# Transposing q and k' on TensorE instead of by DMA, in low-rank attention followed by a GELU MLP

## The chip, the cores and the metric

The kernel runs on one core of a Trainium2 chip. A core has five engines that work side by side, each with its own queue of instructions: TensorE (PE in the profile; its weight loads are the row PEld), VectorE (DVE), ScalarE (ACT), GpSimd (POOL) and SyncE (SP). Sixteen DMA engines move data; here they are fed from the queues of SP and POOL, and once from ACT's. Matmuls write into PSUM, which has 8 banks. The metric is the device time of one execution in microseconds (us), smaller is better.

## The reference

Eight batches of attention with 8 heads, 1024 tokens and head size 64. Keys and values are first projected along the sequence from 1024 to 64 by two matrices E and F, so that each head has only 64 keys. The result goes through an MLP with the sigmoid form of GELU.

```python
k_proj = np.einsum('ks,bhsd->bhkd', E, k)          # (8, 8, 64, 64), "k'"
v_proj = np.einsum('ks,bhsd->bhkd', F, v)
scores = (1/8) * np.matmul(q, k_proj.transpose(0, 1, 3, 2))
attn = softmax(scores)
x = np.matmul(attn, v_proj)                        # then (8192, 512): heads side by side
h = x @ w_in                                       # 512 -> 2048
out = (h * sigmoid(1.702 * h)) @ w_out             # 2048 -> 512
```

## The kernel before, in words

The 8192 tokens are cut into 16 blocks of 512 (`j`), two to a batch (`b`). A block passes through these steps, and the short names are those of the written order:

- `ld` and `lq` load k, v and q of a batch from POOL's queue, with the change of type to bf16 on the way (`load_kv` L58, `load_q` L70).
- `pj` projects k and v of a batch (L674); `kb` and `vq` copy the two results out of PSUM.
- `qd` and `kd` transpose q and k' of a batch by DMA transposes from SP's queue (L239, L684), so that the head size lies along the partitions, as the scores need it. `qda` and `qdb` do the same for half a batch.
- `sc` computes scores from the transposed q and k' (through `eight`, L249), `ex` the exponential on ScalarE, `su` the sums (L652), `va` the products with v' (L249). The sums go through `den`, `ga`, `rc`, `sr` and `sb`: to memory, back, inverted and broadcast over the partitions (`rbc`), with four small or middling DMAs from SP's queue. `mv` multiplies the products with them into `xT` (L646).
- `u0` to `u3` with `P1` to `P7` are the first matrix of the MLP (L610), done by Strassen's scheme with 7 products in place of 8; `c` and `d` are its copies and sums, `g` its GELUs. `xs`, `gs` are sums of its inputs. `F1` to `F7` are the second matrix by the same scheme (L504), with `Fc`, `Fo` and `Fd` behind them; `st` stores the output.

Blocks 0 and 1 go another way in the opening: block 0 has its own functions (`scores0`, `tok0`, `x_tr0`, `ffn1`, then `O` for the second matrix), block 1 has `tk`, `tr`, `tm`, `xt`, `xc` for its attention and `L`, `Lg` for the first matrix, both without Strassen's scheme. While block 0 waits for data, `warm` matmuls on zeros fill TensorE's queue. The second half of batch 0's q is transposed on TensorE by `q_tr` (L230).

What stands in which order on each engine is written out by hand, in lists of step names. `OPEN` covers the start up to block 4, `STEPS` is repeated for each block from 4 to 12, `TAIL` ends it. In `OPEN` and `TAIL` a word is name@block, with PSUM banks behind a colon and the engine of the copy behind a slash; in `STEPS`, `name+3` is that step of the block three further on. `BANK` and `ON_ACT` give banks and copying engine where a word has none. Waits follow from the data: an instruction waits for those whose results or buffers it needs, and holds up what is behind it on its engine. Steps that belong to a batch run only for even blocks (`BATCH`).

Two tiny copies on POOL into `held` put its queue on hold: in `ld` it waits for the transposed q (L677), in `lq` for `rbc` (L696), so that the large loads start only then.

Of the kernel before, what the change touches and what calls it, by code (L numbers as in the profile page):

```python
# [10 lines left out]
BF16 = mybir.dt.bfloat16  # L11
# [6 lines left out]
def kernel(ctx, tc, q, k, v, E, F,  # L18
                                                     moe_w_in, moe_w_out, out):
    nc = tc.nc  # L20
# [69 lines left out]
    for i in range(8):  # L90
        load_w_in(i)
    load_q(0, JB)
    for i in range(4):
        sl = slice(i * FC // 4, (i + 1) * FC // 4)
        nc.gpsimd.dma_start(out=w_out_sb[:, sl, :], in_=w_out_v[:, sl, :])
# [127 lines left out]
    def q_tr(g):  # L223
        def go():
            if 0 not in qT:
                qT[0] = att.tile([P, J, HP, P], BF16, name="qT")
            t_ps = f_tile([P, 2, HP, P], BF16)
            for jj in range(2):
                for p in range(HP):
                    nc.tensor.transpose(t_ps[:, jj, p, :],  # L230
                                        qt[0][:, 2 * g + jj, 2 * p:2 * p + 2, :].rearrange("s t d -> s (t d)"), ident)
            nc.vector.tensor_copy(qT[0][:, 2 * g:2 * g + 2], t_ps)
        return go

    def q_dma(b, j0=0, n=J):
        def go():
            if j0 == 0:
                qT[b] = att.tile([P, J, HP, P], BF16, name="qT")
            nc.sync.dma_start_transpose(out=qT[b][:, j0:j0 + n].rearrange("r j p s -> r (j p) s"),  # L239
                                        in_=qt[b][:, j0:j0 + n].rearrange("s j h d -> s (j h d)"))  # L240
        return go
# [67 lines left out]
    def ffn1(j, fc, ts=slice(0, TB)):  # L309
        if j not in gts:  # L310
            gts[j] = gT
        n = ts.stop - ts.start
        h_ps = f_tile([P, n])
        for kc in range(KC):
            nc.tensor.matmul(h_ps, w_in_sb[:, kc, fc * P:(fc + 1) * P], xT[j][:, kc, ts],
                             start=(kc == 0), stop=(kc == KC - 1))
        nc.scalar.activation(gts[j][:, fc, ts], h_ps, AF.Gelu_apprx_sigmoid)
# [58 lines left out]
    def ffn2_ops(j):  # L376
# [8 lines left out]
        wi.5@1/D sc.1@1:5,6 sc.0@1:7,4 ex.0.0@1 ex.1.1@1 ex.0.1@1 O.2.0@0:3 O.3.0@0:2 O.2.1@0 tk.0.1@1:0 qda@2  # L385
        O.3.1@0 ex.1.0@1 tk.0.0@1:5 tr.0.1@1 tm.0.1@1 tk.1.0@1:0 tk.1.1@1:7 tr.0.0@1 tm.0.0@1 O.1.0@0:6 O.1.1@0
        O.1.2@0 xt.0@1:4 gt@6 tr.1.0@1 tk.3.0@1:1 tr.1.1@1 tm.1.1@1 O.3.2@0 O.3.3@0 tk.2.1@1:5 tk.2.0@1:7
        xc.0@1/A wi.4@1 O.1.3@0 tm.1.0@1 tr.2.0@1 xt.1@1:0 tm.2.0@1 oc.3@0/D ws.1@1 tr.3.0@1 xc.1@1/A O.0.0@0:7
        ws.0@1 O.0.1@0 O.2.2@0 tk.3.1@1:4 tr.2.1@1 tm.2.1@1 O.0.2@0 tm.3.0@1 tr.3.1@1 tm.3.1@1 oc.1@0/D xt.2@1:5
        xc.2@1/A O.0.3@0 xt.3@1:1 xc.3@1/A O.2.3@0 ws.2@1 L.5@1:0 L.0@1:6 oc.0@0/D L.15@1:2 Lg.0@1 oc.2@0/A  # L390
        Lg.5@1 gt@3 L.4@1:4 L.1@1:7 pj@2:5 Lg.4@1 L.14@1:0 kb@2/A Lg.15@1 L.11@1:1 Lg.14@1 Lg.1@1 kd@2 L.2@1:6
        L.7@1:4 ws.3@1 L.9@1:3 vx.0@2 vq.0@2/D vx.1@2 vq.1@2/D Lg.7@1 Lg.11@1 ws.4@1 qdb@2 Lg.9@1 L.6@1:5
        L.8@1:4 L.10@1:7 Lg.8@1 Lg.2@1 L.3@1:1 L.12@1:3 L.13@1:2 ws.5@1/D lq@2 Lg.10@1 Lg.3@1 Lg.6@1 Lg.12@1
        Lg.13@1 gs1.0@1 sc.1@3:3,6 sc.0@2:0,1 gs2.0@1 sc.0@3:4,7 F1.0@1:2 ex.1.1@3 ex.0.1@2 gs1.1@1 gs4.0@1
        F1.1@1 gs2.1@1 gs3.0@1 Fc1@1:1/D F5.0@1:5 ex.1.0@3 ex.0.1@3 F5.1@1 F6.0@1 ex.0.0@3 ex.0.0@2 su@3:0,6
        den.0@3/A sc.1@2:3,4 tk.0.0@2:7 F2.1@1 ex.1.0@2 tk.1.0@2:0 ex.1.1@2 Fc3@1/A den.1@3/D tr.0.0@2 tm.0.0@2
        gs4.1@1 tk.0.1@2:3 tr.1.0@2 tm.1.0@2 tr.0.1@2 tm.0.1@2 tk.1.1@2:7 tr.1.1@2 F2.0@1 tm.1.1@2 F6.1@1 s0.1@0
        tk.2.1@2:4 tk.2.0@2:0 xt.0@2:6 s0.0@0 xt.1@2:3 F3.1@1 tr.2.1@2 tr.2.0@2 xc.0@2/A tm.2.0@2 tm.2.1@2 ga@3
        gs3.1@1 tk.3.0@2:0 F3.0@1 xc.1@2/A tk.3.1@2:6 tr.3.0@2 Fc2@1/A xt.2@2:3 tm.3.0@2 xc.2@2/A tr.3.1@2
        tm.3.1@2 gt@4 Fo0@1/A rc@3 xs.0@2 Fd2@1 F7.1@1 u0.P1@2:7 u0.c1@2:5/D xt.3@2:3 u1.P5@2:6 u1.P1@2:0  # L400
        u1.c1@2:2/D F7.0@1 xc.3@2/A xs.1@2 u0.P2@2 Fd1@1 u0.P5@2:4 u0.c3@2/D sr@3 u1.P2@2 u0.P6@2 u1.P6@2 F4.0@1
        u1.c3@2/D u0.c2@2/D u1.P3@2 ld@2 u2.P1@2:3 u0.g11@2 u3.P1@2:7 xs.2@2 u1.c2@2/A qd@4 u1.P7@2 u1.d2@2
        u1.g11@2 xs.3@2 F4.1@1 u0.P3@2 u1.g12@2 u2.c1@2:0/A sb@3 u1.d1@2 u2.P2@2 u0.d2@2 Fo1@1/A u3.c1@2:6/A
        u0.P7@2 u3.P2@2 u3.P5@2:4 u2.P5@2:1 u3.P6@2 u2.P6@2 u0.d1@2 u1.g22@2 u3.c3@2/D u3.P3@2 u3.g11@2 u0.g22@2
        u0.g12@2 pj@4:7 u3.c2@2/A u2.c3@2/A gs1.0@2 u3.P7@2 u2.g11@2 u3.d2@2 u2.c2@2/D gs3.0@2 gs2.0@2 u2.P7@2
        u1.P4@2 u3.g12@2 u2.P3@2 kb@4/A u3.d1@2 u0.P4@2 kd@4 u2.d1@2 F1.0@2:3 u1.g21@2 u2.d2@2 F1.1@2 u2.g22@2
        u3.g22@2 u2.g12@2 vq.1@4/A u0.g21@2 gs1.1@2 u3.P4@2 u2.P4@2 vq.0@4/A Fc1@2:1/A u3.g21@2 u2.g21@2
        va.1@3:2,7 va.0@3:4,5 gs2.1@2 mv.1.0@3 mv.0.0@3 F6.1@2 F2.0@2 mv.0.1@3 xs.0@3 mv.1.1@3 F2.1@2 sc.1@4:4,5
        sc.0@4:2,0 F6.0@2 ex.1.1@4 xs.1@3 gs3.1@2 Fc2@2/D F5.0@2:7 st1@1 st0@1 Fo0@2/D ex.0.1@4 ex.0.0@4
        ex.1.0@4 F5.1@2 F7.1@2 sc.0@5:3,6 sc.1@5:0,5 ex.0.0@5 su@4:4,2 den.1@4/A gs4.0@2 F7.0@2 ex.0.1@5  # L410
        den.0@4/D Fc3@2/D u0.P1@3:2 u1.P5@3:3 u0.P5@3:4 ex.1.0@5 u0.c1@3:6/A u1.P1@3:0 u0.c3@3/A gs4.1@2 xs.2@3
        u0.P6@3 Fd1@2 u0.c2@3/D F3.0@2 u1.c3@3/D ex.1.1@5 gt@2 ga@4 u1.c1@3:5/D u0.P3@3 F3.1@2 Fd2@2 u1.P6@3
        gt@5 u0.d2@3 rc@4 u1.c2@3/A ld@4 u0.P2@3 xs.3@3 u1.P2@3 u0.P7@3 u0.g11@3 F4.1@2 u1.P3@3 u1.P7@3 u0.d1@3
        u0.P4@3 u2.P1@3:7 F4.0@2 u1.d2@3 su@5:4,3 sr@4 u1.g11@3 pj@6:0 u1.d1@3 sb@4 Fo1@2/D u3.P1@3:2 u1.g12@3
        u1.P4@3 den.0@5/A u1.g22@3 u0.g22@3 den.1@5/D u2.c1@3:3/A u0.g12@3 kb@6/D u2.P6@3 u0.g21@3 gs1.0@3
        gs2.0@3 u2.P5@3:1 u3.P5@3:6 u3.c1@3:4/A vq.0@6/A u2.c3@3/A u3.c3@3/D u3.P6@3 u2.P2@3 u2.c2@3/A u2.P3@3
        gs3.0@3 vq.1@6/A u3.c2@3/A u3.P3@3 u2.g11@3 lq@4 u2.d2@3 u3.P2@3 u3.g11@3 u2.P7@3 u1.g21@3 u3.d2@3
        u3.P7@3 u3.d1@3 u3.g12@3 u2.g12@3 va.0@4:2,0 va.1@4:1,6 u2.d1@3 mv.0.1@4 mv.0.0@4 u2.g22@3 u3.g22@3
        F1.0@3:5 F1.1@3 u3.P4@3 kd@6 u3.g21@3 ga@5 gs1.1@3 u2.P4@3 mv.1.0@4 u2.g21@3 Fc1@3:1/A gs2.1@3 mv.1.1@4
        u1.P1@4:7 F5.0@3:0 u1.c1@4:6/A qd@6 xs.0@4 F5.1@3 rc@5 F6.1@3 F2.1@3 F2.0@3 u1.P2@4 u1.g11@4 F6.0@3  # L420
        sc.0@6:7,3 sc.1@6:4,2 ex.1.0@6 st1@2 xs.1@4 sr@5 u1.P6@4 xs.2@4 st0@2 xs.3@4 gs3.1@3 gs4.1@3 Fc3@3/D
        sb@5 gs4.0@3 ex.1.1@6 F3.0@3 F3.1@3 u1.c2@4/A Fc2@3/D Fo0@3/D ld@6 ex.0.0@6 F7.0@3 u1.P5@4:4 F7.1@3
        u1.P7@4 u2.P1@4:7 u1.c3@4/D ex.0.1@6 u0.P1@4:2 u1.P3@4 u0.P5@4:5 u0.c1@4:3/A gt@7 Fd1@3 Fd2@3 u0.P6@4
        u1.d2@4 u3.P1@4:0 u0.c3@4/D u0.c2@4/D u3.c1@4:4/A u0.P2@4 u1.g12@4 u0.P3@4 u0.g11@4 u0.d2@4 F4.0@3
        u3.P6@4 F4.1@3 u3.P2@4 u1.d1@4 u3.c2@4/D gt@1 u3.g11@4 u0.P7@4 Fo1@3/A u0.d1@4 u1.g22@4 u0.g22@4
        u2.P5@4:2 u1.P4@4 u2.c1@4:5/D u3.P5@4:0 u3.P7@4 u3.c3@4/D u2.P6@4 u1.g21@4 u0.g12@4 u2.c3@4/A u0.P4@4
        u3.d1@4 u3.P3@4 u3.P4@4 u2.c2@4/D u0.g21@4 u2.P2@4 u3.g21@4 u2.g11@4 u3.d2@4 u2.P7@4 u2.P3@4 va.0@5:0,3
        su@6:1,4 den.0@6/A u2.d1@4 den.1@6/A u2.g22@4 mv.0.1@5 u2.d2@4 va.1@5:6,7 u2.P4@4 u3.g12@4 gs1.0@4 lq@6
        u2.g21@4 st0@3
    """.split()  # L430
    STEPS = """
        F1.0 pj+4 mv.1.1+1 u3.g22 mv.0.0+1 u2.g12 mv.1.0+1 xs.0+1 gs2.0 ga+2 sc.1+3 sc.0+3 kb+4 F1.1 u1.P1+1
        vq.0+4 vq.1+4 gs1.1 xs.1+1 gs2.1 Fc1 kd+4 ex.1.1+3 u1.P5+1 F2.1 ex.1.0+3 u1.c3+1 F2.0 Fo0 xs.3+1 F6.0
        u1.c1+1 gs3.1 F5.0 u0.P5+1 u1.P6+1 F6.1 st1-1 ex.0.0+3 ex.0.1+3 gt+4 rc+2 sr+2 u0.P1+1 sb+2 qd+4 ld+4
        lq+3 u0.c1+1 xs.2+1 F5.1 u1.P3+1 gs3.0 Fc2 gs4.1 u0.c3+1 u0.P2+1 u1.c2+1 u1.d2+1 gs4.0 F7.0 u1.P2+1
# [40 lines left out]
    def step(name, j, banks=(), eng=None):  # L476
# [217 lines left out]
        elif i == "lq":  # L694
            if b >= 2:
                nc.gpsimd.tensor_copy(held[:, 0], rbc[j - 1][:1, 0, :1])  # L696
            load_q(b + 1)
        else:
            raise KeyError(name)
# [98 lines left out]
```

## Time and profile before

| What | us |
|---|---|
| Timed runs | 464.88, 466.00, 466.42; median 466.0 |
| Profiled execution, its own time | 464.02 |
| its span, first to last instruction | 462.2 |
| TensorE, busy | 455.6 |
| VectorE, busy | 343.6 |
| ScalarE, busy | 307.8 |
| GpSimd, busy | 82.5 |

How to read the profile: matmuls follow one another in a pipeline, and the mean duration of one (219 ns for 128 columns, 273 for 256) is longer than the distance from one start to the next. What one costs in a full queue is read from the starts. A view of waits lists the engine and line that waited, what it waited for, the time in total, how often, and the longest. In the timeline and in the chain of waits a row has the start and the duration in us, then engine, line and what was done; `x8` are eight instructions in a row. The stages' rows have start and end, length, the busy time of PE, PEld, DVE, ACT and POOL with their instruction counts, the granted clock, and the mean share and the GB/s of DMA.

DMA in the profiled execution, from the page: the software queue (POOL's loads) took 56.7% of the 16 engines' span, the hardware queue of SP 34.5%. DMA transposes: 8 of q (11.7 us from issue to landing) and 7 of k' (3.3 us).

### The profile page before, as it was taken

To read this page: it belongs to the slowest core of one execution; us is meant where nothing else is said; L and a number is where in the kernel's file an instruction comes from. 1 tells how busy PE (TensorE), PEld (TensorE's weight loads), DVE (VectorE), ACT (ScalarE), POOL (GpSimd) and SP (SyncE) were. 2 spreads that over 40 slices of the span, in tenths; PEclk is the share of its full clock that TensorE was granted. 3 is DMA by queue.
4 is the path that set the end of the run, shared out by engine and by line. 5 is a ranking of instruction groups with operands and counts; after the bars stand their busy time and mean duration, and the time that the engine had idled before them with its cause. 6 is when DMAs were issued, how large, how long until landed. Compare 5 with 4: busy or idle time off the path is not lost.

```text
span 462.2 us, 10631 instructions
## 1 busy us (share of the span) xinstructions
PE 455.6 (99%) x4378; PEld 361.9 (78%) x4378; DVE 343.6 (74%) x616; ACT 307.8 (67%) x539; POOL 82.5 (18%) x111
## 2 busy tenths in 40 slices
PE   8999999999999999999999999999999999999997
PEld 4644448877778788887888788787888888888886
DVE  4547957887785977878687876888788796977771
ACT  2665367686767967769585776958677676737462
POOL 7463107052013201041010601015000000000000
PEclk9999999999999999999999999999999999999999
DMA  9999999999999978999988987989664123242022
GB/s 167 200 187 207 182 174 156 197 241 199 148 219 254 158 145 135 223 127 157 162 152 188 156 126 143 211 158 155 138 128 116 45 79 88 94 94 92 1 91 92
DMA packets 133731, 69.19 MB, mean 150 GB/s; under 512 B 98484, under 2 KB 123060, under 8 KB 133684
## 3 DMA queue, kind: packets, MB, share of 16 engines
q0 software_dynamic: 86496, 29.37, 56.7%
q1 hardware_dynamic: 47108, 38.90, 34.5%
q8 instruction: 34, 0.56, 0.5%
q10 hardware_dynamic: 80, 0.26, 0.2%
q14 instruction: 13, 0.11, 0.1%
HBM read 72.88 MB, written 16.99 MB: 194 GB/s over the span
## 4 chain that ended last, share of the span: by engine, by line
PE 87%; DMA 8%; DVE 2%; POOL 1%; issue 1%; ACT 0%; SPq 0%; DVEq 0%; POOLq 0%; ACTq 0%
PE k_ps L504 39%; PE k_ps L610 35%; PE k_ps L249 3%; PE k_ps L550 3%; PE k_ps L556 3%; DMA v_sb<-in_v_dram 3%; PE k_ps L674 2%; DMA w_in_sb<-in_moe_w_in_dram 2%; DMA rbc<-rdr 2%; DMA rdr<-rc 1%; DVE sg L357 1%; PE k_ps L652 1%; POOL k_sb L58 0%; POOL v_sb L58 0%; PE k_ps L567 0%
## 5 line engine op out<-in xcount | busy, mean ns | idle before, releaser
L504 PEld LDWEIGHTS <-sg 128*128 128x128 bf16 x960 | 93.6, 98 | 12.0 <-issue 1.3
L610 PEld LDWEIGHTS <-late 128*128 128x128 bf16 x896 | 87.4, 98 | 11.3 <-issue 1.2
L489 DVE TENSOR_TENSOR q_even<-k_ps,q_even 128x512 f32<-128x512 f32 x112 | 74.6, 687 | 22.7 <-PE k_ps L610 21.0
L610 PE MATMUL k_ps<-xw,late 128*128 128x256 bf16 x672 | 90.2, 273 | 0.0
L504 PE MATMUL k_ps<-tw,sg 128*128 128x256 bf16 x720 | 89.1, 273 | 0.0
L626 ACT ACTIVATE gT<-k_ps 128x512 bf16<-128x512 f32 x112 | 63.8, 596 | 32.8 <-PE k_ps L610 32.2
L504 PEld LDWEIGHTS <-gT 128*128 128x128 bf16 x720 | 68.7, 98 | 15.9 <-issue 8.2
L626 ACT ACTIVATE gT<-q_even 128x512 bf16<-128x512 f32 x112 | 66.2, 630 | 19.1 <-DVE q_even L489 19.0
L610 PEld LDWEIGHTS <-w_in_sb 128*128 128x128 bf16 x672 | 65.5, 98 | 9.3 <-issue 1.7
L610 PE MATMUL k_ps<-xT,w_in_sb 128*128 128x256 bf16 x448 | 64.7, 273 | 0.5 <-DVE xT L646 0.4
L504 PE MATMUL k_ps<-w_out_sb,gT 128*128 128x256 bf16 x480 | 59.3, 273 | 0.0
L70 POOL DMA_DIRECT2D q_sb<-in_q_dram x56 | 49.0, 901 | 40.5 <-DMA qT<-q_sb 18.1
L374 DVE TENSOR_TENSOR sg<-gT 128x1024 bf16<-128x1024 bf16 x60 | 40.9, 681 | 6.6 <-ACT gT L626 3.3
L614 ACT COPY k_ps<-k_ps 128x512 f32<-128x512 f32 x40 | 23.0, 575 | 22.7 <-PE k_ps L610 20.5
L646 DVE TENSOR_TENSOR xT<-k_ps,rbc 128x512 bf16<-128x512 f32 x52 | 32.8, 683 | 3.7 <-PE k_ps L249 1.4
L489 DVE TENSOR_TENSOR o_sb<-k_ps,u_sb 128x512 f32<-128x512 f32 (+1 forms) x31 | 20.6, 668 | 19.1 <-PE k_ps L504 14.4
L638 ACT ACTIVATE expT<-k_ps 128x512 bf16<-128x512 f32 x60 | 32.4, 602 | 3.1 <-PE k_ps L249 3.0
L610 PE MATMUL k_ps<-xT,late 128*128 128x256 bf16 x224 | 33.3, 273 | 0.0
L610 PE MATMUL k_ps<-xw,w_in_sb 128*128 128x256 bf16 x224 | 31.6, 273 | 0.0
L504 PE MATMUL k_ps<-w_out_sb,sg 128*128 128x256 bf16 x240 | 30.6, 273 | 0.0
L504 PE MATMUL k_ps<-tw,gT 128*128 128x256 bf16 x240 | 29.1, 273 | 0.0
L618 DVE COPY q_even<-k_ps 128x512 f32<-128x512 f32 x37 | 25.2, 683 | 5.2 <-PE k_ps L610 5.1
(122 smaller groups left out, 522.3 us busy)
## 6 DMA issues: line engine op xcount, KB each, us to landing
out_dram<-o_sb SPq DMA_DIRECT2D x30, 512.0 KB, 5.0
rbc<-rdr SPq DMA_DIRECT2D x26, 512.0 KB, 6.2
k_sb<-in_k_dram POOLq DMA_DIRECT2D x7, 1024.0 KB, 12.3
q_sb<-in_q_dram POOLq DMA_DIRECT2D x56, 128.0 KB, 6.6
v_sb<-in_v_dram POOLq DMA_DIRECT2D x7, 1024.0 KB, 17.5
w_in_sb<-in_moe_w_in_dram POOLq DMA_DIRECT2D x8, 256.0 KB, 11.3
w_out_sb<-in_moe_w_out_dram POOLq DMA_DIRECT2D x4, 512.0 KB, 11.5
v_sb<-in_v_dram POOLq DMA_DIRECT2D x4, 256.0 KB, 10.4
```

What stands on the lines that cost most here:

```text
L70: nc.gpsimd.dma_start(out=qt[b][:, j], in_=qv[:, j])
L249: nc.tensor.matmul(outs[i][r.start + c:r.start + c + w], lhsTs[i][ri, c:c + w], rhss[i][ri], start=True, stop=True)
L374: nc.vector.tensor_tensor(t[i - 1], in0, in1, op=ALU.add if i == 1 else ALU.subtract)
L489: nc.vector.tensor_tensor(out_, in0, in1, op=ALU.add)
L504: nc.tensor.matmul(dst, x[:, k_, t * P:(t + 1) * P], w[:, k_], start=(first and k_ == 0), stop=(final and k_ == FH - 1), skip_group_check= ...
L550: nc.tensor.matmul(live[f"O{n}", j], gts[j][:, fc, n * P:(n + 1) * P], w_out_sb[:, fc, :], start=(fc == 0), stop=(fc == FC - 1))
L610: nc.tensor.matmul(live[h, j][:, r], a[:, k_, f:f + P], w[:, k_], start=(i in (1, 5) and r == 0 and k_ == 0), stop=(i in (2, 3, 4) and r = ...
L614: copy(new(B_, [P, 2, TH]), live[A, j])
L618: copy(u2, live[G, j])
L626: nc.scalar.activation(out_, in_, AF.Gelu_apprx_sigmoid)
L638: nc.scalar.activation(expT[j][:, 2 * n + t, :], live[f"S{n}{t}", j], AF.Exp, scale=scale)
L646: nc.vector.tensor_tensor(x_of(j)[:, n, :], live[f"V{p[1]}{t}", j], rbc[j][:, n, :], op=ALU.mult)
```

## The change

q and k' of batches 1 to 7 are transposed by matmuls with the identity matrix. `qt.0` and `qt.1` transpose the q of one block, 8 transposes of 128x128 each into one PSUM bank, and `qc.0`, `qc.1` copy them to `qT`, which is now kept per block. `kt` transposes k' of a batch with 4 transposes, and `kc` copies it to `kts`; `kb` now copies all 128 partitions of the projection. `qd`, `qda`, `qdb` and `kd` are gone, and with them the hold in `ld`; the hold in `lq` is now on the newest `rbc`. `q_tr` writes block 1's part alone. The three lists, the banks and the copying engines are written anew. In the opening, the last eighth of w_in is loaded behind the second half of q; ffn1's first two tiles are begun while the last heads are still missing; the sums of w_in are made in two halves. The end stores its second half in one piece.

```diff
-    for i in range(8):
+    for i in range(7):
         load_w_in(i)
     load_q(0, JB)
+    load_w_in(7)
...
-    def q_dma(b, j0=0, n=J):
-        def go():
-            if j0 == 0:
-                qT[b] = att.tile([P, J, HP, P], BF16, name="qT")
-            nc.sync.dma_start_transpose(out=qT[b][:, j0:j0 + n].rearrange("r j p s -> r (j p) s"),
-                                        in_=qt[b][:, j0:j0 + n].rearrange("s j h d -> s (j h d)"))
...
+    def ffn1_kc(fc, kc):
+        if fc not in begun:
+            begun[fc] = f_tile([P, TB]), []
+        begun[fc][1].append(kc)
+        nc.tensor.matmul(begun[fc][0], w_in_sb[:, kc, fc * P:(fc + 1) * P], xT[0][:, kc, :],
+                         start=(kc == 0), stop=(kc == KC - 1))
+
+    def ffn1_begin(fc0, fc1, n):
+        for fc in range(fc0, fc1):
+            ffn1_kc(fc, n - 1)
...
     OPEN = """
-        wi.5@1/D sc.1@1:5,6 sc.0@1:7,4 ex.0.0@1 ex.1.1@1 ex.0.1@1 O.2.0@0:3 O.3.0@0:2 O.2.1@0 tk.0.1@1:0 qda@2
...
+        O.3.0@0:7 wi.4@1 sc.1@1:2,6 sc.0@1:1,0 ex.0.1@1 ex.0.0@1 O.2.0@0:3 O.2.1@0 O.3.1@0 tk.1.0@1:5 ex.1.0@1
...
+        ws.1@1 O.1.3@0 xc.2@1/A xc.3@1/A O.0.3@0 L.6@1:5 L.7@1:7 L.8@1:3 oc.1@0/D L.2@1:4 Lg.7@1 Lg.8@1 Lg.6@1
+        qt.0@2:6 pj@2:2 oc.0@0/A qc.0@2/A vq.0@2/D L.5@1:5 L.1@1:0 L.11@1:7 L.0@1:3 vq.1@2/A gt@4 Lg.2@1 Lg.5@1
...
     STEPS = """
-        F1.0 pj+4 mv.1.1+1 u3.g22 mv.0.0+1 u2.g12 mv.1.0+1 xs.0+1 gs2.0 ga+2 sc.1+3 sc.0+3 kb+4 F1.1 u1.P1+1
-        vq.0+4 vq.1+4 gs1.1 xs.1+1 gs2.1 Fc1 kd+4 ex.1.1+3 u1.P5+1 F2.1 ex.1.0+3 u1.c3+1 F2.0 Fo0 xs.3+1 F6.0
-        u1.c1+1 gs3.1 F5.0 u0.P5+1 u1.P6+1 F6.1 st1-1 ex.0.0+3 ex.0.1+3 gt+4 rc+2 sr+2 u0.P1+1 sb+2 qd+4 ld+4
...
-        u3.P2+1 u2.d1+1 Fd2 u3.P7+1 u0.P4+1 u2.g22+1 u2.P4+1 u3.g11+1 u0.g21+1 u3.d1+1 u2.P3+1 u3.P4+1 va.0+2
-        u2.g21+1 u3.d2+1 u2.d2+1 mv.0.1+2 su+3 u3.g21+1 va.1+2 den.0+3 den.1+3 u3.g12+1 st0
+        F1.0 u3.g22 F1.1 qt.0+3 u3.g21 mv.1.1+1 qt.1+3 u3.g12 kt+3 mv.0.0+1 Fc1 F2.1 u2.g12 qc.0+3 kc+3 pj+4
+        qc.1+3 sc.0+3 lq+2 gs1.1 gs2.1 gs3.1 xs.0+1 ga+2 sc.1+3 F2.0 u0.P1+1 F6.1 vq.0+4 gs3.0 F6.0 kb+4
+        ex.1.0+3 u1.P1+1 vq.1+4 gs4.0 ex.1.1+3 ex.0.0+3 u0.c1+1 xs.1+1 Fo0 u1.P5+1 ex.0.1+3 u0.P5+1 rc+2 F5.0
...
+        u3.P7+1 u2.P4+1 su+3 ld+3 u3.d2+1 u2.g22+1 va.1+2 va.0+2 den.1+3 u3.d1+1 den.0+3 u2.g21+1 mv.1.0+2
+        u3.P4+1 mv.0.1+2
...
     TAIL = """
-        gs4.1@15 Fo0@15/A st0h@15 F4.1@15 F4.0@15 f3.1@15 f3.0@15 Fo1@15/A st4.1@15 fd2.1@15 st2.1@15 fd2.0@15
-        st2.0@15
+        Fd1@15 fd2.0@15 F4.1@15 F4.0@15 f3.1@15 st0h@15 st2.0@15 fd2.1@15 Fo1@15/A st1@15 st2.1@15
...
-    ON_ACT = ("Fc1", "Fc2", "den.0", "den.1", "kb", "u0.c1", "u0.c2", "u1.c1", "u2.c1", "u2.c3", "u3.c2", "vq.0",
-              "vq.1")
+    ON_ACT = ("Fc1", "Fc2", "Fc3", "Fo0", "den.1", "u0.c2", "u0.c3", "u1.c1", "u1.c2", "u2.c1", "u2.c3", "u3.c2",
+              "u3.c3")
...
         elif i == "ld":
-            nc.gpsimd.tensor_copy(held[:, 1], qT[b][:1, J - 1, 0, :1])
...
         elif i == "kb":
-            tmps["kb"] = att.tile([KP, H, D], BF16, name="k_b")
-            copy(tmps["kb"], live["PJ", j][LO])
-        elif i == "kd":
-            nc.sync.dma_start_transpose(out=kts[b % 2], in_=tmps["kb"].rearrange("k h d -> k (h d)"))
+            tmps["kb"] = att.tile([P, H, D], BF16, name="k_b")
+            copy(tmps["kb"], live["PJ", j])
+        elif i == "kt":
+            new("KT", [P, HP, P], BF16)
+            for n in range(HP):
+                nc.tensor.transpose(live["KT", j][:, n], tmps["kb"][:, 2 * n:2 * n + 2].rearrange("k t d -> k (t d)"),
+                                    ident)
+        elif i == "kc":
+            copy(kts[b % 2], live["KT", j][:, :, :KP])
+        elif i == "qt":
+            if j not in qT:
+                qT[j] = att.tile([P, HP, JB, P], BF16, name="qT")
+            new(f"Q{t}", [P, 2, JB, P], BF16)
+            for e in range(2):
+                for n in range(JB):
+                    nc.tensor.transpose(live[f"Q{t}", j][:, e, n],
+                                        qt[b][:, c * JB + n, 4 * t + 2 * e:4 * t + 2 * e + 2]
+                                        .rearrange("s t d -> s (t d)"), ident)
+        elif i == "qc":
+            copy(qT[j][:, 2 * t:2 * t + 2], live[f"Q{t}", j])
...
         elif i == "lq":
             if b >= 2:
-                nc.gpsimd.tensor_copy(held[:, 0], rbc[j - 1][:1, 0, :1])
+                nc.gpsimd.tensor_copy(held[:, 0], rbc[max(rbc)][:1, 0, :1])
...
+    x_tr0(2, 0, 2, AC)
     tok0(3, 0)
     tok0(3, 1)
-    warm(1, True)
-    x_tr0(2, 0, 2, AC)
+    ffn1_begin(0, 2, 1)
+    ffn1_begin(0, 2, 2)
     x_tr0(3, 0, 1, DV)
     x_tr0(3, 1, 1, AC)
...
+    ffn1_begin(0, 2, 3)
+
+    halves = slice(0, DH // 2), slice(DH // 2, DH)
+    for fc in range(FC):
+        ffn1(fc)
+        if fc in (8, 13):
+            for i in (2, 3, 0, 1):
+                w_in_sums(i, cols=halves[fc > 8])
+        if fc in (11, 12):
+            q_tr(fc - 9)()
```

## The prediction

> **What bounds the kernel now.** I read the page first, then whom TensorE waits for, then the chain of waits over one batch, the busy time by stage, and TensorE's timeline where the change touches it. The page (parts 1 and 2) shows TensorE busy almost everywhere at the full clock, and the DMA engines busy too for two thirds of the span:
>
> ```profile
> PE 455.6 (99%) x4378; PEld 361.9 (78%) x4378; DVE 343.6 (74%) x616; ACT 307.8 (67%) x539; POOL 82.5 (18%) x111
> PE   8999999999999999999999999999999999999997
> PEclk9999999999999999999999999999999999999999
> DMA  9999999999999978999988987989664123242022
> ```
>
> Since the ends of matmuls are modelled, I asked whether TensorE waits. Its list of waits is short, 2.8 us in all, and only the second line lies after the first 21 us:
>
> ```profile
> PE k_ps L144 <- DVE u_sb L109: 1.5, 1, 1.5
> PE k_ps L610 <- DVE xT L646: 0.4, 1, 0.4
> PE k_ps L184 <- DMA v_sb<-in_v_dram: 0.4, 1, 0.4
> ```
>
> The chain of waits over one batch is matmuls only. From one batch's projection to the next (210.27 to 264.11) are 53.84 us, and 8 matmuls of 256 columns take 0.87 us, 109 ns each. The stages (PE, PEld, DVE, ACT, POOL, clock, DMA share, GB/s) say that this pace does not depend on the DMA engines: a share of 0.96 or of 0.61 makes no difference.
>
> ```profile
> 210.27 1.85 PE k_ps L674 x16
> 212.12 0.56 PE k_ps L249 x16
> ...
> 264.11 1.85 PE k_ps L674 x16
> ```
>
> ```profile
> 210.30:264.10 53.80, 53.80 (x546) 45.12 (x548) 42.23 (x73) 38.89 (x68) 9.10 (x12) 1.00 0.96 158
> 317.90:371.80 53.90, 53.90 (x553) 45.22 (x560) 42.14 (x73) 38.99 (x68) 0.09 (x1) 1.00 0.61 114
> ```
>
> So TensorE's queue is full from 22 us to the end. What is added to it lengthens the kernel one for one, and what is taken off the DMA engines gives nothing unless a TensorE wait goes with it. One rule says otherwise: the Trainium skill, "Perfetto Trace Analysis", section Identifying the Most-Contended Engine, calls matmul busy time a bad measure and has headroom judged by the weight loads' busy share. By it, 78% would leave 22% of 462 us, some 100 us, in which transposes could hide. I follow the starts instead: they stand 109 ns apart with no holes.
>
> **The change part by part.** *Transposes added.* Each block from 2 to 15 (14 of them) gets `qt.0` and `qt.1`, 8 transposes each: 224. Each batch from 1 to 7 gets `kt`, 4 transposes: 28. In sum 252 of 128x128 bf16. The trace has the same operation, `q_tr` at L230:
>
> ```profile
> 34.09 0.61 PE L230 MATMUL k_ps<-ident,q_even 128*128 128x128 bf16 x8
> 34.54 1.03 PE L315 MATMUL k_ps<-xT,w_in_sb 128*128 128x512 bf16 x4
> 35.40 0.61 PE L230 MATMUL k_ps<-ident,q_even 128*128 128x128 bf16 x8
> 35.85 1.03 PE L315 MATMUL k_ps<-xT,w_in_sb 128*128 128x512 bf16 x4
> 36.97 0.63 PE L249 MATMUL k_ps<-qT,kt 64*32 64x512 bf16 x16
> ```
>
> Eight occupy TensorE from 34.09 to 34.54, 56 ns each; the 219 ns that the groups give as mean is latency, not pitch. 252 x 0.0556 = 14.0 us. Two rules of the Trainium skill, "TensorE: Matmul & The Clock Gate", speak against the change more strongly. Part 4 (PE-mode transpose) gives about 275 ns per transpose inside a kernel: 69 us. Part 2 (Back-to-back issue gap) gives 81 ns for 128 columns with a weight load each: 20.4 us. The row is of this kernel, with weight loads, so 14.0 is taken; 20.4 stays as the upper end, and no row supports 69.
>
> *Groups of split matmuls.* Projection, scores, values and sums use parts of the array, and entering such a group costs: the 8 matmuls of L610 should give way at 417.48 + 0.87 = 418.35, but L249 starts at 418.44, 0.09 us later.
>
> ```profile
> 417.48 1.04 PE L610 MATMUL k_ps<-xw,late 128*128 128x256 bf16 x8
> 418.44 0.62 PE L249 MATMUL k_ps<-expT,vq 64*32 64x512 bf16 x16
> ```
>
>  Counting unbroken groups in the orders: OPEN 12 before, 16 after; TAIL 1 and 2; STEPS 2 and 2 (one holds `pj`). Five more, 0.5 us. The other matmuls are the same in kind and number, but for one `warm` of 512 columns that goes (it is in the opening's sum).
>
> *Opening.* Before ffn1, TensorE's timeline is:
>
> ```profile
> 19.53 0.62 PE L184 MATMUL k_ps<-v_sb,late 128*128 128x128 bf16 x8 [0.35 <-DMA v_sb<-in_v_dram]
> 20.93 0.38 PE L144 MATMUL k_ps<-zeros 128*128 128x512 bf16 x1
> 21.95 12.30 PE L315 MATMUL k_ps<-xT,w_in_sb 128*128 128x256 bf16 x64
> ```
>
> The last `v` lands at 19.5 us in both, since its loads are issued first. Before, TensorE then has waits and a `warm` until L315 starts at 21.95 and ffn1 ends at 35.85 + 4 x 0.216 = 36.71. After, six of ffn1's 64 matmuls (1.3 us) are begun in those waits. Worked along DVE's and ACT's copies, the last x_tr0 is copied at about 22.5, then 58 x 0.216 + 0.9 (q_tr) = 13.4: ffn1 ends at 35.95, so 0.75 less. The scores of block 1 also stand 0.26 behind ffn1 (36.71 to 36.97), waiting for q_tr's copies on DVE, which trail the sums of w_in (L357, waits of 7.7 us on w_in's DMA); the new place of those sums and `O.3.0` ahead of the scores cover that. Together -1.0. `load_w_in(7)` moved behind four q loads lands where the last of those did, near 33.5 us; its first user, fc = 14, comes near 34.2. Nothing, but with 0.7 us of cover.
>
> *Waits that go.* At 130.4 TensorE stands 0.6 us for xT (L646), behind rbc's DMAs that share SP's queue with transposes; at 382.6 it stands 0.2. Both go with luck: -0.8.
>
> *Waits that come, in the opening.* In TensorE's order `pj@2` now stands after all O, the tk and xt, four L and `qt.0`: 35.95 + 13.8 + 0.65 + 0.9 + 0.9 + 3.45 + 0.45 = 56.1. It needs v of batch 1, issued at 39.11 and 18.3 us to landing, 57.4; before, `pj` began at 57.57. Nothing ahead of that load gets lighter. So +1.0, with 12 L matmul groups queued behind it. `pj@4` is as tight (k and v of batch 2, issued near 60 and after 14 us, against 74.5): 0 to 1.5, taken as 0.
>
> *Waits that come, in the steady order.* `sc.0` and `sc.1` need `qc.0`, `kc`, `qc.1` from DVE, where a 128x1024 copy is 680 ns (L232). In odd blocks, where no `pj` stands between, TensorE has qt.1 0.45 + kt 0.22 + F2.1 0.87 = 1.5 us between qt.0 and sc.0. DVE has, from va's end, the last of u3.d1, den.0, four mv (2.48 us for four), qc.0, kc: about 4.3 us against TensorE's 4.2 up to sc.0, and qc.1 0.6 later. From nothing to 0.6 us a block; taken 0.2 in the five odd blocks, +1.0; the bad end is 0.5 in all twelve, 6.
>
> *Copies.* 28 qc and 7 kc make per batch 4 x 0.68 + 0.3 = 3.0 us on DVE; `ON_ACT` moves five copies a block to ScalarE and den.0, u0.c1, kb and vq to DVE. DVE 42.2 - 6.9 + 4.3 + 3.0 = 42.6, ScalarE 38.9 + 2.2 = 41.1, of a batch of 55.8. Both stay under TensorE: nothing.
>
> *Queues.* SP loses 8 q and 7 k' transposes (landing 11.7 and 3.3 us); behind them stood gather, rdr and rbc, which TensorE already does not feel but once. POOL loses the hold on qT (104.8 us in five waits) ahead of the k and v loads; `lq` still holds, now on the newest rbc. Its eight q loads are issued in 7 us and land within 7 more, and `qt` wants them a block (27 us) later: nothing, cover about 12 us. The end (3.3 us from the last matmul to the span's end) swaps two stores of 256 KB for one of 512 (2.2 and 2.6 us to landing in the last stage): 0, give or take 0.3.
>
> *Sum.* The profiled execution took 464.0 us (span 462.2). 464.0 + 14.0 + 0.5 - 1.0 - 0.8 + 1.0 + 1.0 = 478.7. The profiled execution lies 2.0 below the median of the three timed runs, so 480.7.
>
> **The rivals.** *The price alone, plus small waits* (chance 0.68): as summed, its own range 477.5 to 484.
> *TensorE's price plus a poorly fitting order* (0.20): the q chain (qt, copy, scores) costs 0.5 us in each of 12 blocks and the loads 2 to 3 in the opening, 485 to 488. For it: the 4.3 against 4.2 us above. Against: an order with three engines above 67% runs here with one wait.
> *Dearer transposes* (0.06): 81 ns, +6.4, 487.
> *TensorE has real slack* (0.04), the other side: the transposes slip into holes of the matmul stream, as the weight loads' 78% would allow, and the opening's 1.0 and the waits' 0.8 are kept: 466.0 - 1.8 + 0.5 = 464.7, just faster by 0.3%. It decides when a transpose costs under some 1 ns, or when a batch period of 53.84 shrinks by 2 us with the DMA transposes gone. Against both: the pitch of 56 ns in L230, and the period that stays at 53.8 with DMA at 0.61.
> *It does little* (0.02): another part of the order saves what the transposes cost, within 0.3% of 466; only the 22 us before ffn1 could hold so much, and they wait for k, q and v, which load as before.
>
> **How the numbers follow.** Likeliest 480.7. About 0.3% (1.4 us) is what a measurement of this kernel can tell from no change. Low end 477.0: no new wait (476.7 profiled), a timed run only 0.9 above the profile, as the lowest of the three, and the end's 0.3 in favour. High end 487.0: into the second and third case. Faster 0.04, same 0.02, slower 0.94.
>
> **What would show it.** Right: TensorE 252 instructions more, transposes with starts 56 ns apart; a batch period near 55.9 (53.84 + 36 x 0.0556) with DMA share far below 0.96; ffn1 ending about 36.0; a wait on v's DMA near 56. Wrong: a period still at 53.8 (slack was real), or over 57 with TensorE waiting for the copies (the order fits badly), or transposes 80 ns apart.

## The result, and the profile after

The changed kernel takes 481.12 us (median of four, 480.77 to 481.3) against 465.74 for the kernel before (median of four): a ratio of 1.033, interval 1.0311 to 1.035, so 15.4 us slower. The profiled execution took 481.29 us, with a span of 479.5.

The page of the changed kernel, parts 1 and 2, as shown of before:

```profile
PE 471.6 (98%) x4613; PEld 375.7 (78%) x4621; DVE 347.9 (73%) x633; ACT 325.1 (68%) x561; POOL 81.2 (17%) x105
...
PE   8999999999999999999999999999999999999996
...
PEclk9999999999999999999999999999999999999999
DMA  9999999859913299166983299451950505132013
```

TensorE is as full as it was, with more in it: 243 weight loads more, which are the 252 transposes less one `warm` and less 8 matmuls of ffn1, whose first two tiles are no longer cut in halves (the matmul counts differ by 235 only, since 8 records are missing from the trace). The DMA row, which stood at seven or more for two thirds of the span, has holes from 96 us on. TensorE's list of waits is still short (1.8 us after the first line), only what it waits for is different:

```profile
PE k_ps L145 <- DVE u_sb L110: 1.5, 1, 1.5
PE k_ps L570 <- ACT expT L641: 0.5, 1, 0.5
PE k_ps L585 <- ACT gT L562: 0.5, 1, 0.5
PE k_ps L507 <- ACT k_ps L521: 0.4, 1, 0.4
PE k_ps L185 <- DMA v_sb<-in_v_dram: 0.2, 1, 0.2
PE k_ps L553 <- DMA w_out_sb<-in_moe_w_out_dram: 0.2, 1, 0.2
```

The chain of waits over one batch now has the transposes of q (L698) and of k' (L688) in it, and two projections (L677) are 55.84 us apart, where they were 53.84:

```profile
278.52 1.85 PE k_ps L677 x16
...
305.48 0.89 PE k_ps L698 x16
306.38 0.22 PE k_ps L688 x4
...
332.59 0.89 PE k_ps L698 x16
...
334.36 1.84 PE k_ps L677 x15
```

Sixteen transposes take 0.89 us and four take 0.22: 56 ns each, and 36 of them are the 2.0 us by which the batch grew. The stages (PE, PEld, DVE, ACT, POOL, clock, DMA share, GB/s) show that the DMA engines were relieved, from a share near 0.97 to 0.79, while TensorE stays busy through the whole batch:

```profile
222.60:278.40 55.80, 55.80 (x581) 47.23 (x580) 42.70 (x75) 40.27 (x71) 8.88 (x12) 1.00 0.79 134
```

### The profile page after: what moved, and what is told of

Its sections match the earlier page's. It is cut to its first block, busy times and chain, and to the rows that moved or that the text cites. A ratio compares the mean times of both kernels' runs of the same rounds, so it can differ in the third digit from the quotient of the medians.

```text
span 479.5 us, 11084 instructions
## 1 busy us (share of the span) xinstructions
PE 471.6 (98%) x4613; PEld 375.7 (78%) x4621; DVE 347.9 (73%) x633; ACT 325.1 (68%) x561; POOL 81.2 (17%) x105
## 4 chain that ended last, share of the span: by engine, by line
PE 82%; DMA 11%; DVE 3%; ACT 1%; POOL 1%; issue 1%; SPq 0%; DVEq 0%; ACTq 0%; POOLq 0%
PE k_ps L507 36%; PE k_ps L613 33%; DMA w_out_sb<-in_moe_w_out_dram 3%; PE k_ps L559 3%; PE k_ps L242 2%; PE k_ps L677 2%; DMA v_sb<-in_v_dram 2%; DMA w_in_sb<-in_moe_w_in_dram 2%; DMA rbc<-rdr 2%; PE k_ps L698 2%; PE k_ps L553 2%; DMA rdr<-rc 1%; DVE xT L649 1%; DVE sg L376 1%; PE k_ps L655 1%
## 5 line engine op out<-in xcount | busy, mean ns | idle before, releaser
L613 PE MATMUL k_ps<-xw,late 128*128 128x256 bf16 x672 | 95.3, 273 | 0.0
L629 ACT ACTIVATE gT<-q_even 128x512 bf16<-128x512 f32 x112 | 67.8, 629 | 18.8 <-PE k_ps L507 13.7
L507 PEld LDWEIGHTS <-gT 128*128 128x128 bf16 x720 | 69.0, 98 | 12.5 <-issue 4.8
L613 PEld LDWEIGHTS <-w_in_sb 128*128 128x128 bf16 x672 | 64.7, 98 | 12.5 <-issue 4.9
L613 PE MATMUL k_ps<-xT,w_in_sb 128*128 128x256 bf16 x448 | 66.1, 273 | 0.0
L621 ACT COPY q_even<-k_ps 128x512 f32<-128x512 f32 x40 | 23.5, 589 | 24.3 <-PE k_ps L613 24.0
L613 PE MATMUL k_ps<-xw,w_in_sb 128*128 128x256 bf16 x224 | 33.4, 273 | 0.0
L619 ACT COPY q_even<-k_ps 128x512 f32<-128x512 f32 x36 | 21.5, 598 | 10.7 <-PE k_ps L613 10.6
## 6 DMA issues: line engine op xcount, KB each, us to landing
v_sb<-in_v_dram POOLq DMA_DIRECT2D x4, 256.0 KB, 10.7
```

The costliest lines, as they stand in the source:

```text
L507: nc.tensor.matmul(dst, x[:, k_, t * P:(t + 1) * P], w[:, k_], start=(first and k_ == 0), stop=(final and k_ == FH - 1), skip_group_check= ...
L613: nc.tensor.matmul(live[h, j][:, r], a[:, k_, f:f + P], w[:, k_], start=(i in (1, 5) and r == 0 and k_ == 0), stop=(i in (2, 3, 4) and r = ...
L619: copy(u1, live[B_, j])
L621: copy(u2, live[G, j])
L629: nc.scalar.activation(out_, in_, AF.Gelu_apprx_sigmoid)
```

## The experiments

The theory under test is one of price: TensorE's queue is full, so every transpose costs its 56 ns one for one, and taking transposes off the DMA engines gives back only the few waits that they caused. Its rivals: the loss comes from the new order with its waits and copies; or TensorE has slack; or the DMA relief is worth several us and TensorE's price is higher still.

### The transposes of q made twice

```diff
-            for e in range(2):
+            for e in (0, 1, 0, 1):
                 for n in range(JB):
                     nc.tensor.transpose(live[f"Q{t}", j][:, e, n],
```

> The changed kernel, but each qt makes its 8 transposes twice into the same bank; no copy, wait or DMA is added. Price theory (TensorE's queue is full, a transpose costs its 56 ns one for one): 224 x 0.0558 = +12.5 us, 493.6 us. Order theory (the 15 us come from the new order, its waits and copies, and transposes slip into holes): under 484 us.

Measured 492.26 us, ratio to before 1.0579 (1.0557 to 1.06), so 11.1 us above the changed kernel. In the trace the 224 more transposes take 12.5 us by their starts, just their price, and a steady batch grows from 55.84 to 57.63 us, by 1.79 for 32 transposes at 0.0558:

```profile
228.44 1.85 PE k_ps L677 x16
...
286.07 1.85 PE k_ps L677 x16
```

The 1.4 us that the kernel gained on that price are waits that shrank, by the starts: 0.7 between the projections near 57 and 77 us, 0.7 near 194. It reads as the added matmuls giving the copies that TensorE waited for more time; no run tests that reading. One for one, less what they cover. The order theory, under 484, is out.

### The transposes of q left out

```diff
+        elif i in ("qt", "qc") and j >= 4:
+            qT[j] = qT[2 + j % 2]
         elif i == "qt":
```

> The changed kernel without qt and qc from block 4 on; the scores of those blocks read the transposed q of block 2 or 3 instead. 192 transposes and 24 copies fewer. Price theory: 481.1 - 192 x 0.0558 = 470.4 us, and what is left over the kernel before (about 4.7 us) is the 60 other transposes (3.3) and the rest of the new order. Order theory: at most 2 us come back, 479 us. A theory in which a transpose costs more than its pitch (81 ns, or a copy that TensorE waits for) gives 465.5 us or less.

Measured 476.71 us, ratio 1.0236 (1.0218 to 1.0254). Only 4.4 us came back instead of 10.7, so here the price theory missed by 6.3. TensorE's list of waits in this run has a new first line:

```profile
PE k_ps L507 <- ACT k_ps L521: 5.0, 9, 0.7
```

and the timeline of one of the nine places is

```profile
216.86 0.64 ACT L629 ACTIVATE gT<-q_even 128x512 bf16<-128x512 f32 x1
217.56 0.57 ACT L521 COPY k_ps<-k_ps 128x512 f32<-128x512 f32 x1
...
218.18 1.03 PE L507 MATMUL k_ps<-w_out_sb,gT 128*128 128x256 bf16 x8 [0.66 <-ACT k_ps L521]
```

The matmuls of `F2.1` add to the bank that `Fc1` (L521) still has to copy, and `Fc1` stands on ScalarE behind GELUs. In the changed order `qt.0`, `qt.1` and `kt` stand between `F1.1` and `F2.1`, and they fill that time. Without them TensorE waits in the same place, by the starts 0.82 us in one block of a batch and 0.60 in the other, 6.5 us in all nine. The batch period shows that price and wait together are the whole account:

```profile
219.21 1.85 PE k_ps L677 x16
...
274.68 1.85 PE k_ps L677 x16
```

That is 55.47 us, and 55.84 less 32 x 0.0558 plus 0.82 and 0.60 makes 55.47. The order was made with these transposes in it: they are price, and they are also cover, the work that fills the time in which TensorE would otherwise wait.

### The same, with F2.1 moved

```diff
-        F1.0 u3.g22 F1.1 qt.0+3 u3.g21 mv.1.1+1 qt.1+3 u3.g12 kt+3 mv.0.0+1 Fc1 F2.1 u2.g12 qc.0+3 kc+3 pj+4
+        F1.0 u3.g22 F1.1 qt.0+3 u3.g21 mv.1.1+1 qt.1+3 u3.g12 kt+3 mv.0.0+1 Fc1 u2.g12 qc.0+3 kc+3 pj+4
...
-        qc.1+3 sc.0+3 lq+2 gs1.1 gs2.1 gs3.1 xs.0+1 ga+2 sc.1+3 F2.0 u0.P1+1 F6.1 vq.0+4 gs3.0 F6.0 kb+4
+        qc.1+3 sc.0+3 lq+2 gs1.1 gs2.1 gs3.1 xs.0+1 ga+2 sc.1+3 F2.1 F2.0 u0.P1+1 F6.1 vq.0+4 gs3.0 F6.0 kb+4
```

> The changed kernel without q's transposes and copies from block 4 on (as the run that gave back 4.4 of 10.7 us), and F2.1 moved in STEPS from before the scores to behind them. Cover theory: the transposes stood between F1.1 and F2.1 and hid Fc1, the copy that F2.1 needs; with the scores in their place the waits of 0.6 and 0.8 us a block go, 5 us in nine blocks: 471.5 us. If instead the copies or DMAs of the new order hold it, it stays near 476.7.

Measured 473.31 us, ratio 1.0147 (1.013 to 1.0164): 3.4 of the expected 5.2 us. The wait for L521 is gone from the list, and part of it has moved on, to the copy of the transposed k' that the scores need:

```profile
PE k_ps L242 <- DVE kt L691: 1.9, 4, 0.5
```

By the starts this new wait is 0.55 us in one block of each batch, and the period closes again:

```profile
216.99 1.85 PE k_ps L677 x16
...
271.59 1.85 PE k_ps L677 x16
```

That is 54.60 us, and 55.84 less 1.79 plus 0.55 makes 54.60. So the cover theory holds, with the next late step in its place. Of the 10.7 us that the transposes occupy, 7.8 have come back, and at least the 1.9 of the list are in sight. Less the four transposes of k' as well (0.22), and without the 0.55, a batch of the new order would by this sum take 53.83 us, as the kernel before does: in the repeated blocks the order itself neither wins nor loses. No run has the new order with the DMA transposes kept, so for the opening and the end that stays open.

### The kernel before, with idle transposes

```diff
+            if i == 1 and t == 0:
+                d_ps = bank(banks[0] if banks else BANK[n], [P, 8, P], BF16)
+                for r in range(17):
+                    nc.tensor.transpose(d_ps[:, r % 8], w_out_sb[:, 0, :P], ident)
             if i in (1, 5) and t == 0:
                 new(n, [P, 2, MH])
```

> The kernel before, DMA transposes and order kept, with 17 idle transposes (128x128 bf16, of a constant, into the bank that F1 is about to use) ahead of F1 in each of blocks 1 to 15: 255, nothing waits for them. Price theory: 465.7 + 255 x 0.0558 = 480.0 us: the whole loss without the change's order. Slack theory (the weight loads' 78% is the true load of TensorE): 466 to 468 us.

Measured 483.23 us, ratio 1.0402 (1.0366 to 1.0439): +17.4 us, more than the 14.2 expected. The timeline shows where the rest is:

```profile
189.55 1.12 PE L513 MATMUL k_ps<-ident,w_out_sb 128*128 128x128 bf16 x17
190.72 1.03 PE L504 MATMUL k_ps<-w_out_sb,gT 128*128 128x256 bf16 x8
```

From 189.55 to 190.72 are 1.17 us, where 17 x 0.0558 = 0.95. The last transpose of each set stands 0.22 us over its pitch before `F1`, which writes into the same bank, starts: 15 x 0.22 = 3.3, and 14.2 + 3.3 = 17.5. That the shared bank is the reason is likely, but no run parts it from other reasons. The 0.22 belongs to this experiment; the changed kernel's 224 transposes of q show 0.2 us of such time in all. Slack is excluded: this order, without any of the change, has no hole for 255 transposes at this place.

### The kernel before, without DMA transposes

```diff
-            nc.sync.dma_start_transpose(out=qT[b][:, j0:j0 + n].rearrange("r j p s -> r (j p) s"),
-                                        in_=qt[b][:, j0:j0 + n].rearrange("s j h d -> s (j h d)"))
+            qT[b] = qT[0]
...
-            nc.gpsimd.tensor_copy(held[:, 1], qT[b][:1, J - 1, 0, :1])
...
-            nc.sync.dma_start_transpose(out=kts[b % 2], in_=tmps["kb"].rearrange("k h d -> k (h d)"))
+            pass
```

> The kernel before without its 15 DMA transposes and without the hold on them: scores of all batches read batch 0's transposed q and k'. TensorE's work stays the same. Price theory: the DMA relief is worth only the two waits of 0.6 and 0.2 us, so 465.0 us, within 0.3% of before. Relief theory (transposes in the DMA queues slow the kernel, and TensorE's own price is therefore above 15 us): 460 us or less.

Measured 465.36 us against 465.83, ratio 0.9992 (0.998 to 1.0003): no difference that can be told. The hardware queue's share fell from 34.5% to 23.2%, the DMA share of a batch from 0.96 to 0.81, and the batch period (211.93 to 265.76, 53.83 us) did not move:

```profile
210.30:264.10 53.80, 53.80 (x552) 45.16 (x544) 42.06 (x73) 38.87 (x68) 8.93 (x11) 1.00 0.81 131
```

```profile
211.93 1.85 PE k_ps L671 x16
...
265.76 1.85 PE k_ps L671 x16
```

The DMA transposes cost the kernel before nothing that can be measured. That is the whole of what the change could win there.

### The scores split in two

```diff
-        F1.0 pj+4 mv.1.1+1 u3.g22 mv.0.0+1 u2.g12 mv.1.0+1 xs.0+1 gs2.0 ga+2 sc.1+3 sc.0+3 kb+4 F1.1 u1.P1+1
+        F1.0 pj+4 mv.1.1+1 u3.g22 mv.0.0+1 u2.g12 mv.1.0+1 xs.0+1 gs2.0 ga+2 sc.1+3 kb+4 F1.1 sc.0+3 u1.P1+1
```

> The kernel before with one word moved in STEPS: sc.0 behind F1.1, so that in each of the 9 repeated blocks the scores enter the split array twice. Group theory (entering costs 0.09 us and leaving about 0.12, as the changed kernel's traces suggest: two groups of 8 take 0.34 each where one of 16 takes 0.56): +9 x 0.21 = 1.9 us, 467.7 us. With the 0.09 of the prediction alone: +0.8, which is no measurable difference.

Measured 467.21 us against 465.68, ratio 1.0026 (1.0011 to 1.004): +1.2 us by the ratio, 0.5 to 1.9. The trace has 40 groups of split matmuls instead of 31. The timeline of the split kernel, where one of them stands alone:

```profile
213.72 1.05 PE L504 MATMUL k_ps<-w_out_sb,gT 128*128 128x256 bf16 x8
214.70 0.41 PE L249 MATMUL k_ps<-qT,kt 64*32 64x512 bf16 x8
215.04 0.61 PE L610 MATMUL k_ps<-xT,w_in_sb 128*128 128x256 bf16 x4
```

The 8 matmuls before it end their turn at 213.72 + 0.87 = 214.59 and it starts at 214.70; it holds TensorE for 0.34, and two such groups make 0.68 where one group of 16 takes 0.56. So entering costs about 0.1, and a group has 0.12 more that does not grow with its matmuls, put down here to leaving. Nine times the 0.21 is the 1.9 expected, nine times 0.09 is 0.8; the interval of the times holds both. The trace decides for the larger: with two split groups more, a batch takes 54.29 us from projection to projection (265.94 to 320.23) in place of 53.83, 0.23 a group.

### The new opening alone

```diff
-    for i in range(8):
+    for i in range(7):
         load_w_in(i)
     load_q(0, JB)
+    load_w_in(7)
...
+    x_tr0(2, 0, 2, AC)
     tok0(3, 0)
     tok0(3, 1)
-    warm(1, True)
-    x_tr0(2, 0, 2, AC)
+    ffn1_begin(0, 2, 1)
+    ffn1_begin(0, 2, 2)
     x_tr0(3, 0, 1, DV)
     x_tr0(3, 1, 1, AC)
...
+    ffn1_begin(0, 2, 3)
```

with the sums of w_in in halves, as in the change.

> The kernel before with the change's opening of block 0 alone: ffn1 begun while the last heads are missing, w_in's last eighth behind q, w_in's sums in halves. DMA transposes and order stay. Opening theory: ffn1 ends 0.5 us earlier and the scores' wait of 0.26 goes: 465.0 us, at the edge of what can be told. Rival: w_in's last eighth or the halves of the sums come too late for what follows, no gain or a loss of up to 1 us.

Measured 465.56 us against 465.68, ratio 0.9993 (0.9984 to 1.0003): no difference. The timeline of its first projection:

```profile
57.26 0.40 PE L684 MATMUL k_ps<-k_sb,eft 128*64 128x512 bf16 x1
58.15 0.38 PE L684 MATMUL k_ps<-v_sb,eft 128*64 128x512 bf16 x1 [0.48 <-DMA v_sb<-in_v_dram]
```

TensorE comes to the projection of batch 1 at 57.26 and stands there till 58.15 for v: that group takes 2.71 us instead of 1.85. What the opening won is given back at the next load. No version came out ahead of the kernel before: neither of the two parts that were tried in it, the missing DMA transposes and the new opening, gains anything by itself.

### The kernel before, once more

> The kernel before once more, for a second profile. The profiled execution was 464.0 us, below all its timed runs (464.1 to 467.5 by now). If a wait that comes and goes with the landing of a DMA makes the difference, this profile shows a wait of about 1.5 us near 82 us, where VectorE's reciprocal waits for the gathered sums and xs.0 stands behind it, as the runs without DMA transposes and with idle transposes do, and takes about 465.5. If the difference lies outside the span, the span is 462.2 again.

It took 465.56 us with a span of 463.8, so the difference lies in the span. The wait near 82 us is not there; that expectation missed. In its place TensorE's list has others:

```profile
PE k_ps L610 <- DVE xT L646: 0.7, 1, 0.7
...
PE k_ps L610 <- ACT k_ps L614: 0.3, 1, 0.3
PE k_ps L249 <- DVE xT L646: 0.2, 1, 0.2
```

By the starts they stand at 131, 197 and in a group of split matmuls near 105, none of them the same size in the first profile. The order before runs with hardly any margin, and single waits of 0.2 to 1.5 us come and go between executions. Those on xT wait on VectorE for products that need `rbc`, a DMA; what moved each of them was not followed further.

## Why the prediction was right

The forecast was 480.7, the median is 481.12. The mechanism held, TensorE's full queue and 56 ns for each transpose; that the forecast came within 0.4 us is luck, as the last paragraph shows. The terms, against the two first profiles (spans 462.2 and 479.5, 17.3 apart), from the starts of TensorE's instructions:

| Term | Predicted, us | Found, us |
|---|---|---|
| 252 transposes | +14.0 | +14.1 |
| Groups of split matmuls, five more | +0.5 | about +1.1 |
| Opening: ffn1's end and the scores' wait | -1.0 | -0.8 (ffn1 ends at 36.21 for 36.72) |
| Waits that go | -0.8 | -1.3 |
| Waits that come, opening | +1.0 | +2.4 |
| Waits that come, steady order | +1.0 | +0.9 |
| End | 0 | +0.4 |
| Sum | +14.7 | +16.8 of 17.3 |

*What bounds it* was read rightly: starts 109 ns apart without holes, not the weight loads' 78%. (The section that the prediction set against this names MFU, the share of the peak arithmetic rate, beside the weight loads; the prediction left that out, and it was not worked out here.) Idle transposes in the unchanged order cost their full time, and the DMA relief alone was worth nothing measurable.

*The price of a transpose* was the row's, 56 ns. Of the two rules of the Trainium skill that were set against it ("TensorE: Matmul & The Clock Gate"), the 81 ns would have made 20.4 us of it and the 275 ns 69; 252 transposes here took 14.1 by their starts, at a granted clock of 1.0 to the end. The 275 ns are the time that one transpose takes; one took 219 ns here too, but the next started 56 ns after it. And the section with the 81 ns gives about 56 as well, for a matmul that stands alone: here that is the figure of the full queue.

*The groups* were counted rightly (31 and 36 in the traces) and priced too low by half: the prediction had only the entry. The split experiment's trace shows that as much again comes behind it.

*The waits that go* went, but that the DMA transposes in SP's queue had caused them, as the prediction had it, the runs do not show. In the kernel before without DMA transposes the wait of 0.2 us is still there (at 384 us). The one of 0.6 near 130 is gone, but one of 1.5 near 83 has come, as it has with the idle transposes, where the DMA transposes are kept. What causes these two stays open.

*The waits in the opening* were the worst-sized term. `pj@2` did wait for v, as said, but only 0.4 us, because TensorE came to it at 56.9 instead of 56.1: small waits in the second matrix of block 0, of which the list names one for w_out's DMA, had held it for 0.5 already. The rest was not foreseen and is at 69 to 76 us, where scores, exponentials and block 2's attention stand close together. The changed kernel's timeline:

```profile
69.80 1.28 ACT L641 ACT_TABLE_LOAD   x1
...
71.10 2.06 ACT L641 ACTIVATE expT<-k_ps 128x512 bf16<-128x512 f32 x4
...
71.75 0.40 PE L570 MATMUL k_ps<-vx,expT 128*128 128x130 bf16 x4 [0.53 <-ACT expT L641]
...
73.18 1.28 ACT L255 ACT_TABLE_LOAD   x1
...
75.12 0.38 PE L585 MATMUL k_ps<-ident,x_sb 128*128 128x128 bf16 x4 [0.50 <-ACT gT L562]
```

TensorE waits there for an exponential and for a GELU (L562, which starts at 74.47), and each of them stands on ScalarE directly behind a table load of 1.28 us, the change from one function's table to the other's. The new order puts one GELU between block 2's exponentials, so ScalarE changes its table at 69.8, 73.2 and 75.6 us; the kernel before does so at 69.7 and not again until 81.6. The prediction's account of ScalarE had no such loads. Together with the waits before 57 us and v that makes the 2.4. No run takes the GELU out of there, so this cause is read from the timeline alone.

*The steady order* was given 0.2 us in each odd block for the copies of q. The trace has no such wait block after block: the 0.9 is mostly one event at 194 us, 0.5 us for Fc1, which ScalarE could start only after products that had waited 0.8 us for `rbc`'s DMA, and behind it 0.2 for copies of q, made late by the same products. The sum fits, the mechanism named for it does not. That the rate of a batch (55.84, predicted near 55.9) holds no wait at all is what the left-out transposes explain: they stand where the order needs something to do.

*The offset* of 2.0 us between profile and median was taken over as if it belonged to the kernel. It belonged to one execution: the changed kernel's profile lies 0.2 above its median, and the second profile of before lies 0.1 below its own. The sum came out 2.6 short, the offset 2.2 too large, and the two errors cancel, which is luck. Against the second profile of before, the span grew by 15.7, and by that one the sum was 1.0 short. One sum of the prediction is off: the terms of its low end (476.7, plus 0.9, less 0.3) make 477.3, not 477.0.

## What to carry to other kernels

When one engine's queue is full without holes, look for what can be taken off it, not for what can be taken off the others: a transpose that the DMA engines did at no measurable cost became 56 ns of TensorE each, 252 times. Ask for fullness at the starts of instructions, and prove it with idle work in the unchanged order. And a part that has been ordered in is not removed for its price: what stands behind it comes to its own waits earlier, so leaving it out understates it here by more than half, while doubling it comes close.

## What the runs showed that was not expected

A group of matmuls that use part of the array costs about as much again behind its entry as at it: 0.34 us for 8 alone, 0.56 for 16 in one group, and 0.1 before the group. After a transpose into a bank that the next matmul overwrites, that matmul started 0.22 us beyond the pitch, 15 times in 15. Single waits of the kernel before moved by as much as 0.6 us between two profiled executions (a group of 16 split matmuls took 0.56 us in one and 1.14 in the other), so one profile's distance from the median is not a constant to carry over.
